# Loads of q and k on ScalarE's queue, and DMA work spread over the steps, in a threshold-attention and MLP kernel

## The chip, the cores and the metric

One core of one Trainium2 chip. The metric is the device time of one execution, in microseconds (us); the kernel before takes 534.13 us (median of 3 runs, 533.15 to 537.44). "Faster" or "slower" needs 2%.

## The reference, cut to what matters

```python
# q, k, v: (8 batches, 8 heads, 576 rows, 64), float32; tau = 0.02
scores = scale * q @ k^T
scores = where(scores >= max(scores) - tau, scores, -1e9)
attn   = softmax(scores);  x = attn @ v      # regrouped to 4608 x 512
out    = leaky_relu(x @ w_in) @ w_out        # 512 -> 2048 -> 512, slope 0.01
```

## The kernel before

The kernel runs 144 steps, 18 to a batch. A step forms scores of 128 query rows of a pair of heads (TensorE, L331), reduces them (VectorE, L391), thresholds and exponentiates them (GpSimd, ScalarE, VectorE); seven steps later the weights meet v. The MLP of earlier rows fills TensorE in between. q and k are loaded as float32 and split into two float16 halves by ScalarE and GpSimd.

Three things must be turned by 90 degrees by DMA transposes, all issued from the sync queue (SP in the profile): the halves of k (`kst<-ks`) and of q (`qst<-qs`), two of each a batch, and the attention weights (`wt<-w`), nine a batch and thirteen in the last. The same queue issues the loads of k and q and the stores of the result. GpSimd's queue has the loads of v, w_in and w_out. The lines that the change touches:

```python
LOADS = (-4, 3)
WOUT = 0

def load_half(src, store, nm, b, hb):
    m = store[b, hb] = sb.tile([128, 2, 576], FP32, tag=nm, bufs=2, name=nm)
    in_ = ...
    if nm == "km":
        nc.sync.dma_start(out=m, in_=...)                      # L100
    else:
        for f in range(2):
            nc.sync.dma_start(out=..., in_=in_[f])             # L103
...
def turn(nm, b, hb):
    nc.sync.dma_start(out=turned(...), in_=split_tile(...), transpose=True)   # L176
...
for b in range(1, B):
    s0 = 18 * (b - 1)
    for hb in range(2):
        t0 = s0 + (PREP1 if b < 2 else PREP)[hb]               # PREP = (3, 9)
        at(s0 + LOADS[hb], lambda ...: load_half(k, kms, "km", b, hb))
        at(s0 + LOADS[hb] + 1, lambda ...: load_half(q, qms, "qm", b, hb))
        ...
        at(t0 + 4, lambda ...: turn("k", b, hb))
        at(t0 + 7, lambda ...: turn("q", b, hb))
    for i in range(4):
        at(18 * b + i, lambda ...: load_v(b, i))               # GpSimd's queue
for g in range(8):
    at(WOUT + g // 2, lambda g=g: load_w_out(g))               # GpSimd's queue
...
    nc.sync.dma_start(out=uwt[now]..., in_=W_..., transpose=True)   # wt<-w, L540
```

`at(s, f)` runs f at the end of step s.

## Time and profile before

| | before |
|---|---|
| time, median | 534.13 us |
| span of the profiled run, granted clock | 529.1 us, 0.948 |
| TensorE's waits for DMA transposes | 13.7 us (wt) + 9.1 us (turns of q) |
| wt transposes, issue: median / mean / longest | 3.66 / 3.79 / 10.63 us |
| what the sync queue spends on issuing | 433.7 us: 381.4 on 104 transposes, 52.2 on loads and stores |

An issue is the time for which a queue is held by one DMA; landing is counted from its start to its completion. Two more views of before are needed later. First the DMA issues of the page (number, KB each, median us from issue to landing):

```profile
km<-in_k_dram SPq DMA_DIRECT2D x16, 576.0 KB, 4.7
qm<-in_q_dram SPq DMA_DIRECT2D x32, 288.0 KB, 4.7
...
wt<-w SPq DMA_TRANSPOSE x76, 6.6
```

Then the DMA queues of the page (packets, MB, time of their packets as a share of 16 engines' span). One queue, q1, carries all transposes, loads of k and q, and stores; q0 is GpSimd's:

```profile
q1 hardware_dynamic: 266304, 92.03, 90.4%
q0 software_dynamic: 13056, 8.92, 13.2%
```

### The profile page before, as it was taken

To read this page: it belongs to the slowest core of one execution; us is meant where nothing else is said; L and a number is where in the kernel's file an instruction comes from. 1 tells how busy PE (TensorE), PEld (TensorE's weight loads), DVE (VectorE), ACT (ScalarE), POOL (GpSimd) and SP (SyncE) were. 2 spreads that over 40 slices of the span, in tenths; PEclk is the share of its full clock that TensorE was granted. 3 is DMA by queue.
4 is the path that set the end of the run, shared out by engine and by line. 5 is a ranking of instruction groups with operands and counts; after the bars stand their busy time and mean duration, and the time that the engine had idled before them with its cause. 6 is when DMAs were issued, how large, how long until landed. Compare 5 with 4: busy or idle time off the path is not lost.

```text
span 529.1 us, 13454 instructions
## 1 busy us (share of the span) xinstructions
PE 475.8 (90%) x4912; PEld 294.5 (56%) x4912; DVE 464.1 (88%) x1213; ACT 424.6 (80%) x924; POOL 278.6 (53%) x476
## 2 busy tenths in 40 slices
PE   4666887999899997999999988999699999999996
PEld 3323454655565664656565655666455666656673
DVE  4985897999999997999999997999779999999542
ACT  6786888988999887898989897898859888878341
POOL 5575845675577645674567545764546644222000
PEclk9655798999999998999999999999989999999999
DMA  8999999999999999999999999999999999766301
GB/s 248 217 198 241 208 205 206 223 201 207 208 238 206 185 211 202 219 224 226 205 218 198 187 228 216 245 197 212 171 254 181 169 187 180 152 116 135 91 21 59
DMA packets 279425, 101.79 MB, mean 192 GB/s; under 512 B 254272, under 2 KB 266560, under 8 KB 279360
## 3 DMA queue, kind: packets, MB, share of 16 engines
q1 hardware_dynamic: 266304, 92.03, 90.4%
q0 software_dynamic: 13056, 8.92, 13.2%
q8 instruction: 38, 0.62, 0.5%
q14 instruction: 27, 0.22, 0.2%
HBM read 36.70 MB, written 9.44 MB: 87 GB/s over the span
## 4 chain that ended last, share of the span: by engine, by line
DVE 51%; DMA 15%; PE 14%; issue 12%; POOL 5%; ACT 2%; SPq 0%; POOLq 0%; DVEq 0%; ACTq 0%
DVE sf L391 20%; DMA wt<-w 10%; DVE gT L216 9%; DVE P L546 8%; DVE w L536 5%; PE op L236 5%; DMA qst<-qs 4%; PE hp L236 4%; PE sc L331 3%; DVE osb L272 3%; DVE xT L372 3%; POOL P L517 2%; PE pv L362 2%; POOL bb L515 1%; DVE rc L534 1%
## 5 line engine op out<-in xcount | busy, mean ns | idle before, releaser
L391 DVE TENSOR_SCALAR_CACHE_REDUCE sf<-sc 128x576 f32<-128x576 f32 x288 | 205.1, 747 | 15.6 <-PE sc L331 14.2
L551 ACT ACTIVATE w<-P 128x576 f16<-128x576 f16 x288 | 193.8, 674 | 8.6 <-DVE P L546 3.9
L331 PE MATMUL sc<-kst,qst 64*128 64x320 f16 (+1 forms) x1536 | 137.8, 300 | 26.1 <-DVE sf L391 16.2
L516 ACT ACTIVATE P<-sf,bb 128x576 f16<-128x576 f32 x144 | 111.3, 773 | 60.4 <-POOL bb L515 56.2
L236 PE MATMUL hp<-xT,win 128*128 128x256 f16 (+1 forms) x1344 | 152.3, 260 | 0.0
L236 PE MATMUL op<-wout,gT 128*128 128x512 f16 x576 | 150.8, 386 | 1.6 <-DVE osb L272 1.6
L236 PEld LDWEIGHTS <-win 128*128 128x128 f16 x1344 | 118.0, 99 | 44.0 <-issue 3.5
L331 PEld LDWEIGHTS <-qst 64*128 64x128 f16 x1536 | 75.9, 98 | 77.8 <-issue 48.2
L517 POOL TENSOR_SCALAR P<-sf,bb 128x576 f16<-128x576 f32 x139 | 105.9, 762 | 14.3 <-POOL bb L515 0.4
L216 DVE SCALAR_TENSOR_TENSOR gT<-hp,gT 128x512 f16<-128x512 f32 x144 | 98.2, 682 | 14.0 <-ACT gT L250 14.0
L250 ACT ACTIVATE gT<-hp 128x512 f16<-128x512 f32 x144 | 83.6, 581 | 20.5 <-PE hp L236 20.4
L515 POOL TENSOR_SCALAR bb<-mx 128x2 f32<-128x2 f32 x139 | 27.4, 197 | 120.9 <-DVE sf L391 107.7
L546 DVE TENSOR_SCALAR P<-P 128x1152 int16<-128x1152 int16 x144 | 82.0, 570 | 0.0
L236 PEld LDWEIGHTS <-gT 128*128 128x128 f16 x576 | 46.2, 98 | 64.3 <-issue 29.1
L362 PE MATMUL pv<-wt,v 128*64 128x256 f16 (+2 forms) x1000 | 56.8, 253 | 13.9 <-DMA wt<-w 13.7
L362 PEld LDWEIGHTS <-v 128*64 128x64 f16 x1000 | 38.2, 112 | 30.5 <-issue 26.3
L551 ACT ACTIVATION_READ_ACCUMULATOR w<-P 128x1 f32 x288 | 53.9, 187 | 0.0
L164 POOL TENSOR_TENSOR ks<-km,ks 128x320 f16<-128x320 f32 (+1 forms) x56 | 39.9, 733 | 10.8 <-DVE P L546 10.1
L372 DVE TENSOR_TENSOR xT<-pv,wt 128x128 f16<-128x128 f32 x128 | 31.7, 291 | 13.6 <-PE pv L362 13.5
L164 POOL TENSOR_TENSOR qs<-qm,qs 128x576 f16<-128x576 f32 x28 | 35.9, 1282 | 13.6 <-DVE P L546 13.6
L536 DVE TENSOR_SCALAR w<-rc 128x256 f16<-128x256 f32 (+1 forms) x76 | 39.6, 521 | 2.6
L126 POOL DMA_DIRECT2D v<-in_v_dram x32 | 20.6, 644 | 22.9 <-PE sc L331 10.1
(35 smaller groups left out, 211.8 us busy)
## 6 DMA issues: line engine op xcount, KB each, us to landing
km<-in_k_dram SPq DMA_DIRECT2D x16, 576.0 KB, 4.7
qm<-in_q_dram SPq DMA_DIRECT2D x32, 288.0 KB, 4.7
out_dram<-osb SPq DMA_DIRECT2D x36, 256.0 KB, 3.5
v<-in_v_dram POOLq DMA_DIRECT2D x16, 160.0 KB, 6.1
v<-in_v_dram POOLq DMA_DIRECT2D x16, 128.0 KB, 6.3
win<-in_moe_w_in_dram POOLq DMA_DIRECT2D x8, 256.0 KB, 10.1
wout<-in_moe_w_out_dram POOLq DMA_DIRECT2D x8, 256.0 KB, 11.0
wt<-w SPq DMA_TRANSPOSE x76, 6.6
```

Of the source, the lines that this page charges most:

```text
L164: return nc.gpsimd.tensor_tensor(out=dst[:, h], in0=src[:, h], in1=h_[:, h], op=AX.subtract)
L216: nc.vector.scalar_tensor_tensor(out=G.g[u], in0=hp, scalar=0.01, in1=G.g[u], op0=AX.mult, op1=AX.add)
L236: nc.tensor.matmul(out=out_, lhsT=lhsT, rhs=rhs, start=start, stop=stop, skip_group_check=True)
L250: nc.scalar.activation(out=G.g[u], in_=hp, func=AF.Relu, bias=0.0, scale=0.99)
L331: nc.tensor.matmul(out=sc[h][:, cols], lhsT=qt[r, qi, ds(2 * c, 2)].rearrange("d t a b -> d (t a b)")[:, g::2], rhs=rhs, start=(i == 0), s ...
L362: nc.tensor.matmul(out=o_[ds(64 * h, 64)], lhsT=vt[:, pp, h, j, :], rhs=w_[:, :, 4 * h + j, :], start=(j == 0), stop=(j == 4), skip_group_ ...
L391: nc.vector.tensor_scalar(out=sf, in0=sc[h][:, ds(SC0, 576)], scalar1=C, scalar2=None, op0=AX.mult, op1=AX.max, accum_out=mx[:, h : h + 1])
L516: nc.scalar.activation(out=P_[:, 1, :], in_=sB, func=AF.Identity, bias=bb[:, 1:2], scale=1.0)
L517: (nc.vector if s < SPOOL else nc.gpsimd).tensor_scalar(out=P_[:, 0, :], in0=sa, scalar1=1.0, scalar2=bb[:, 0:1], op0=AX.mult, op1=AX.add)
L536: nc.vector.tensor_scalar(out=W_[:, :, 1152:1280].rearrange("p i (h r) -> p i h r", h=2), in0=rc[:, 0:nw, :].unsqueeze(3).to_broadcast([12 ...
L546: anchor[0] = nc.vector.tensor_scalar(out=pi, in0=pi, scalar1=NEG, scalar2=None, op0=AX.max)
L551: nc.scalar.activation(out=uW[ui][:, i, ds(576 * h, 576)], in_=P_[:, h, :], func=AF.Exp, bias=exp_bias, scale=1.0, accum_out=usm[ui][:, i, ...
```

## The change

Its intent: take the loads of q and k off the crowded sync queue, and place loads, turns and the loads of w_out so that few DMAs fall on one step. The diff, cut to its core:

```diff
-    WOUT = 0
-    LOADS = (-4, 3)
+    LOADS = ((-6, 0), (2, 4))
+    TURNS = ((8, 10), (14, 16))
+    VS = (-6, 0, 2, 4)
+    WOUTS = (0, 2, 4, 6, 8, 10, 12, 14)
...
-            nc.sync.dma_start(out=m, ...)
+            nc.scalar.dma_start(out=m, ...)
...
-                nc.sync.dma_start(out=m.rearrange(...)[f], in_=in_[f])
+                nc.scalar.dma_start(out=m.rearrange(...)[f], in_=in_[f])
...
-            at(s0 + LOADS[hb], ... load_half(k, ...))
-            at(s0 + LOADS[hb] + 1, ... load_half(q, ...))
+            at(s0 + LOADS[hb][0], ... load_half(k, ...))
+            at(s0 + LOADS[hb][1], ... load_half(q, ...))
...
-            at(t0 + 4, ... turn("k", b, hb))
-            at(t0 + 7, ... turn("q", b, hb))
+            at(s0 + TURNS[hb][0], ... turn("k", b, hb))
+            at(s0 + TURNS[hb][1], ... turn("q", b, hb))
...
-            at(18 * b + i, ... load_v(b, i))
+            at(18 * b + VS[i], ... load_v(b, i))
...
-        at(WOUT + g // 2, ... load_w_out(g))
+        at(WOUTS[g], ... load_w_out(g))
```

More of the change, by code (lines that the diff above doesn't have):

```diff
@@ L99, in load_half @@
         if nm == "km":
-            nc.sync.dma_start(out=m, in_=in_.rearrange("f p h x -> (f p) h x"))
+            nc.scalar.dma_start(out=m, in_=in_.rearrange("f p h x -> (f p) h x"))
         else:
             for f in range(2):
-                nc.sync.dma_start(out=m.rearrange("(p f) h x -> f p h x", f=2)[f], in_=in_[f])
+                nc.scalar.dma_start(out=m.rearrange("(p f) h x -> f p h x", f=2)[f], in_=in_[f])
     anchor = [None]
@@ L458 @@
             t0 = s0 + (PREP1 if b < 2 else PREP)[hb]
-            at(s0 + LOADS[hb], lambda b=b, hb=hb: load_half(k, kms, "km", b, hb))
-            at(s0 + LOADS[hb] + 1, lambda b=b, hb=hb: load_half(q, qms, "qm", b, hb))
+            at(s0 + LOADS[hb][0], lambda b=b, hb=hb: load_half(k, kms, "km", b, hb))
+            at(s0 + LOADS[hb][1], lambda b=b, hb=hb: load_half(q, qms, "qm", b, hb))
             at(t0 - 1, lambda b=b, hb=hb: hi("k", b, hb))
@@ L471 @@
                             at(t0 + i, lambda nm=nm, h=h, b=b, hb=hb, part=part: after_anchor(lo(nm, b, hb, h, part)), ptick)
-            at(t0 + 4, lambda b=b, hb=hb: turn("k", b, hb))
-            at(t0 + 7, lambda b=b, hb=hb: turn("q", b, hb))
+            at(s0 + TURNS[hb][0], lambda b=b, hb=hb: turn("k", b, hb))
+            at(s0 + TURNS[hb][1], lambda b=b, hb=hb: turn("q", b, hb))
         for i in range(4):
-            at(18 * b + i, lambda b=b, i=i: load_v(b, i))
+            at(18 * b + VS[i], lambda b=b, i=i: load_v(b, i))
     for g in range(8):
-        at(WOUT + g // 2, lambda g=g: load_w_out(g))
+        at(WOUTS[g], lambda g=g: load_w_out(g))
     pv_at = {}
```

## The prediction

> **What bounds the kernel now.** I read the table of engines first, then the busy times in stretches, then the waits, then the sync queue in order of time.
>
> ```profile
> PE 475.8 (90%) x4912; PEld 294.5 (56%) x4912; DVE 464.1 (88%) x1213; ACT 424.6 (80%) x924; POOL 278.6 (53%) x476
> ```
>
> No engine is idle for long. I cut the steady part at the first score reduction (DVE, L391) of every sixth of the 144 steps. A batch is 18 steps, so three stretches are one batch; these are the batch from 187.3 us:
>
> ```profile
> 187.30:210.00 22.70, 19.76 (x174) 11.48 (x173) 18.97 (x51) 18.09 (x40) 10.23 (x19) 0.92 1.30 203
> 210.00:228.70 18.70, 18.70 (x208) 11.56 (x207) 18.31 (x50) 16.87 (x39) 13.74 (x22) 1.00 1.15 220
> 228.70:247.50 18.80, 18.65 (x199) 11.60 (x198) 18.70 (x52) 16.80 (x38) 11.62 (x19) 1.00 1.07 209
> ```
>
> Columns after the length: PE, PEld, DVE, ACT, POOL busy us, clock, DMA, GB/s. In the second and third stretch VectorE and TensorE are both full: a floor of 18.7 us for six steps. The first stretch is 4.0 us longer with no more VectorE work. Who held it:
>
> ```profile
> PE pv L362 <- DMA wt<-w: 13.7, 8, 4.5
> ...
> PEld L331 <- DMA qst<-qs: 10.6, 5, 3.2
> PE sc L331 <- DMA qst<-qs: 9.1, 4, 2.9
> ```
>
> (The list of waits: us in total, times, longest.) PE's waits for transposed tiles are 13.7 + 9.1 = 22.8 us in twelve places. The PEld line is mostly the same wait seen by the weight loads, and I don't add it. The place in the stretch above:
>
> ```profile
> 201.13 1.62 PE L331 MATMUL sc<-kst,qst 64*128 64x320 f16 x12 [2.94 <-DMA qst<-qs]
> ```
>
> ```profile
> 202.79 0.76 DVE L391 TENSOR_SCALAR_CACHE_REDUCE sf<-sc 128x576 f32<-128x576 f32 x1 [2.93 <-PE sc L331]
> ```
>
> PE stood for 2.94 us for the turned q, and VectorE behind it for 2.93. The chain of waits says the same ("190.78 10.31 DMA qst<-qs"). Why was q late? The sync queue before it:
>
> ```profile
> 179.94 2.71 SPq L176 DMA_TRANSPOSE kst<-ks  x1
> 182.71 0.58 SPq L100 DMA_DIRECT2D km<-in_k_dram  x1
> 183.39 0.58 SPq L273 DMA_DIRECT2D out_dram<-osb  x1
> 184.14 5.15 SPq L540 DMA_TRANSPOSE wt<-w  x1
> 189.34 1.34 SPq L103 DMA_DIRECT2D qm<-in_q_dram  x2
> 190.78 4.78 SPq L176 DMA_TRANSPOSE qst<-qs  x1
> 195.73 5.28 SPq L540 DMA_TRANSPOSE wt<-w  x1
> 201.10 0.60 SPq L273 DMA_DIRECT2D out_dram<-osb  x1
> 201.87 7.76 SPq L540 DMA_TRANSPOSE wt<-w  x2
> 209.69 0.58 SPq L100 DMA_DIRECT2D km<-in_k_dram  x1
> ```
>
> Each entry starts within 0.2 us of the end of the one before: the queue never waits for data, it is behind. The turn of q at 190.78 us was placed in step 16 of its batch and is issued in step 1 of the next, three steps late; it lands 0.04 us before PE's wait ends. So the steady state has two floors of nearly equal height: VectorE with TensorE at 3 x 18.7 = 56.1 us a batch, and the issue time of the sync queue. From medians that is 9 x 3.66 (wt) + 2 x 2.79 (kst) + 2 x 3.46 (qst) + 2 x 0.58 + 4 x 0.64 (loads) + 4.5 x 0.59 (stores) = 51.8 us, and about 21 gaps of 0.13 us make 54.6; in the batch above, with its slow transposes, I sum 57.6 us of issuing. When contention lifts it over 56, the queue falls behind and PE pays.
>
> **What the Trainium skill says.** "DMA: Bandwidth & Descriptors", section "Issuing engines are not separate DMA queues": DMAs of all engines run on the same 16 DMA engines, so another issuer saves only issue time. Issue time is what is short here (the rows above), so that is the right currency; bandwidth is not gained. "Perfetto Trace Analysis", section "DMA Instruction — HWDGE (DVE, Sync)": the descriptor generator is shared and locked for exclusive use, and the recorded time includes the wait for the lock. This trace has one hardware issuer alone and can't show it; it is my main risk. "ScalarE: Activation LUTs", section "What ACT_TABLE_LOAD costs": about 1283 ns; the trace agrees, 1.28 us at 0.80 us. "Advanced Engine Details and Errata", section "Sequencer Loop": engine instructions are queued, so a sequencer can be ahead of its engine. The trace agrees: ScalarE's sequencer passed the semaphore for a split (L154) at 139.59 us; that split started at 140.93, 1.34 us later.
>
> **The change part by part.**
>
> 1. Loads leave the sync queue. Per batch 2 x 0.58 + 4 x 0.64 = 3.7 us and six gaps (0.4): the 54.6 become 50.5, and the bad 57.6 some 53.5. Both are under 56.1, so the backlog drains and the transposes go out near their steps. The bytes stay, so contention stays.
>
> 2. Turns. k moves from steps 7 and 13 to 8 and 14; q stays at 10 and 16 (in the first batch prepared so, the first k turn stays at 8 and the first q turn moves from 11 to 10). The attention weights' transposes fall on odd steps, so all turns now lie between them. The queue stood behind no unready turn in the steady part, so this alone is worth little: 0 to 2 us overall.
>
> 3. Loads of w_out go from two a step in steps 0 to 3 to one every second step to step 14. The first wt was issued at 25.43 us, landed 16.57 us later beside them, and PE waited 4.51 us for it at 42.14. w_out pieces land about 1.5 us apart (29.41, 30.96, 32.68); four of the six that landed from 32.68 to 41.14 fall away from this window: about 6 us earlier, more than the 4.5 us wait. But k and q of the next batch now go out early and take some of that. I count 4 us.
>
> 4. The steady gain. Of the 22.8 us, 4.5 is the first wt (part 3) and 1.25 + 0.76 lie at 466 and 490 us, where nothing is loaded any more. 16.3 us remain, in six batches. I count 13, since v loads and both k and q still share the first six steps with the turn of q.
>
> 5. ScalarE pays. It gets the 3.7 us a batch. Its order is exp, exp, split, load; at the end of a step the sequencer is 1.3 us ahead, as much as a pair of q loads (1.28). So most is hidden if an issue still takes 0.6 us. But in the first six steps ScalarE is busy 17.83 of 19.00 us in an undisturbed batch (130.4 us), and 1.28 + 0.58 + 1.28 = 3.1 us fall just there. If half is exposed, 1.6 us meets 1.2 us of idle time and the 1.34 us by which ScalarE's relu usually precedes its reader on VectorE: nearly nothing comes through. I count 0.4 us a batch, 3 us.
>
> 6. The start. ScalarE's queue has the table load first:
>
> ```profile
> 0.80 1.28 ACT L70 ACT_TABLE_LOAD   x1 [0.80 <-PEq L593]
> 2.10 0.20 ACT L70 ACTIVATE warm<-warm 128x1 f32<-128x1 f32 x1
> 4.79 1.26 ACT L154 ACTIVATE ks<-km 128x640 f16<-128x640 f32 x2 [2.50 <-DMA km<-in_k_dram]
> ```
>
> The first load went out from the sync queue at 0.81 us; behind the table load it goes out at about 2.1 us. Everything at the start hangs on it: +1.3 us.
>
> Sum: 534.1 - 4 - 13 - 1 (turns) + 3 + 1.3 = 520.4 us, -2.6%.
>
> **Rivals.**
>
> A. The lock. If ScalarE's issue waits until the sync queue's transpose has generated its descriptors (3 to 5 us, and the sync queue issues nearly always), a load waits some 2 us on average, the second of a q pair again. Per batch in the first six steps 2 x 5 + 2.6 = 12.6 us instead of 3.1, less 3 x 1.3 hidden and 2.5 slack: 6 us of stall a batch, some 36 in six. Then 520 - 3 + 36 = about 553; milder, 530 to 545. For it: the skill's wording. Against it: the DMA page names the saving of issue time as the one use of a second issuer, and loads on the sync queue took 0.58 us right behind a transpose whose bytes were still in flight. I give a clearly lengthened issue one chance in four.
>
> B. The transposes are slowed by bandwidth, not by their queue. They take 3.1 us at best and 5.2 beside loads. If loads from a separate queue slow them as much or more, the queue drains less and the turn of q stays late: half of the 13 us is lost, about 527. For it: the DMA share over 1 in all steady stretches. Against it: the same stretches move 200 to 235 GB/s, while the first loads land 288 KB in 0.73 to 0.84 us, about 350 to 400 GB/s. One in four.
>
> C. Another engine is the bound anyway. VectorE's idle time from 12.6 to 483.7 us sums to 32.6 us, but only the 22.8 us of DMA waits are the change's to win: 534.1 - 22.8 = 511 us is the limit. ScalarE at 51.8 us a batch plus 3.7 makes 55.5, just under the floor of 56.1, so a third engine then stands level with the other two.
>
> **Range and chances.** Without A and B 514 to 522; with B 523 to 530; with A 530 to 555. The middle lands at 521, the range of 8 in 10 is 512 to 545. Faster by over 2% means under 523.4: half. Slower means over 544.8, only full A: 0.16. Within: 0.34.
>
> **What would show it.** Part 1: gaps of over 1 us in the sync queue, and turns of q issued in step 16 or 17. Parts 3 and 4: PE's waits for qst and wt under 6 us together, and stretches of six steps of 19 us. Part 5: ScalarE's load issues at 0.6 us; if their median is over 2 us, A holds and I am wrong on the sign. Part 6: the first split of k at about 6.1 us in place of 4.79. If the wt transposes' median issue rises over 4 us, B holds.

## The result, and the profile after

The changed kernel takes 565.0 us (median of 4 runs, 561.48 to 570.24), beside 535.79 us for the kernel before. The ratio is 1.052 (95% interval 1.043 to 1.061): slower. Ratios here are the mean time of one kernel's fast runs over that of the other's in the same rounds, so not quite the ratios of the medians quoted. The profiled run of the changed kernel was its slowest, 570.24 us (span 568.4); its three fast runs have spans of 559.6 to 563.4 us. (One core runs here; "slow" means a run over 1.5% above the fastest of the same kernel.) Where a size matters I also use an experiment that isolates the queue (act_only). A second series of the changed kernel:

**after_again** (the same kernel once more).

> The changed kernel once more, unchanged, for a profile in the fast state: 561 to 566 us by the earlier fast runs, with the same shape: wt transposes issuing in over 10 us in the first six steps of a batch, load issues on ScalarE of 0.4 to 0.7 us.

Measured: 564.2 us (554.56 to 577.41), ratio 1.041 (1.031 to 1.050). The loss repeats. Two of its four runs were slow, and its profile again fell in one of them:

```profile
PE pv L364 <- DMA wt<-w: 48.4, 15, 11.9
...
PE sc L333 <- DMA qst<-qs: 8.1, 1, 8.1
```

Now the trace. Line numbers in the changed kernel are two higher. Its waits (us in total, times, longest):

```profile
PE pv L364 <- DMA wt<-w: 52.7, 16, 12.5
...
PE sc L333 <- DMA qst<-qs: 1.9, 1, 1.9
```

The waits for the turned q, 9.1 us before, have all but gone in this run (after_again has one of 8.1 us). The waits for the attention weights' transposes went from 13.7 to 52.7 us. Together 22.8 became 54.6 us, 31.8 more; the span is 39.3 us longer. (TensorE was also busy for 484.2 us in place of 475.8, at a granted clock of 0.927 in place of 0.948.)

The same cut as the prediction's, by every sixth step (length, then busy us of PE, PEld, DVE, ACT, POOL, clock, DMA share, GB/s), in the batch that lost most:

```profile
147.40:168.80 21.40, 18.33 (x167) 11.14 (x166) 18.69 (x50) 17.90 (x39) 9.59 (x18) 0.92 1.23 155
168.80:202.70 33.90, 21.18 (x206) 12.60 (x205) 19.50 (x50) 17.49 (x40) 13.63 (x22) 0.80 1.11 154
202.70:221.40 18.70, 18.70 (x231) 12.44 (x230) 18.60 (x50) 16.05 (x37) 12.58 (x20) 1.00 1.12 209
```

The last stretch is at the floor of 18.7 us. The middle one is 15 us above it, with hardly more work on VectorE; the time of the DMA packets fills the 16 engines (share 1.11) and yet they move 154 GB/s, where the stretches of before that the prediction shows moved 203 to 220. What was issued there, each in order of time: the sync queue, then ScalarE's, then TensorE's wait.

```profile
149.93 3.91 SPq L542 DMA_TRANSPOSE wt<-w  x1
153.93 0.60 SPq L275 DMA_DIRECT2D out_dram<-osb  x1
154.69 31.65 SPq L542 DMA_TRANSPOSE wt<-w  x3
```

```profile
150.40 0.63 ACTq L105 DMA_DIRECT2D qm<-in_q_dram  x1
151.07 0.87 ACTq L105 DMA_DIRECT2D qm<-in_q_dram  x1
156.57 0.38 ACTq L102 DMA_DIRECT2D km<-in_k_dram  x1
163.46 0.64 ACTq L105 DMA_DIRECT2D qm<-in_q_dram  x1
165.99 0.61 ACTq L105 DMA_DIRECT2D qm<-in_q_dram  x1
```

```profile
182.80 1.28 PE L364 MATMUL pv<-wt,v 128*64 128x64 f16 x40 [12.51 <-DMA wt<-w]
```

The row of three spans 31.65 us: the first transpose was issuing for 15.51 us and the second for 12.14, where the median is 3.7. The third went out when all these loads had landed, and took 3.18. In each case the weights to be turned had been ready before the issue began, so this is not a wait for data. k was issued while both pieces of the q before it were in flight (they landed at 160.84 and 163.26 us), and the next q while k was (178.62 us); three v loads came from GpSimd meanwhile. TensorE stood 12.51 us for a transposed tile. The landing times of that window tell how slow everything was:

```profile
qm<-in_q_dram ACTq DMA_DIRECT2D x4, 288.0 KB, 14.4
km<-in_k_dram ACTq DMA_DIRECT2D x1, 576.0 KB, 22.0
...
wt<-w SPq DMA_TRANSPOSE x4, 13.9
```

Over the whole run the loads land later, the wt transposes at the median do not (6.7 beside 6.6 us); it is the tail that grew (longest issue 15.5, longest landing 28.1 us):

```profile
km<-in_k_dram ACTq DMA_DIRECT2D x16, 576.0 KB, 6.7
qm<-in_q_dram ACTq DMA_DIRECT2D x32, 288.0 KB, 8.4
...
wt<-w SPq DMA_TRANSPOSE x76, 6.7
```

And the queues of the page:

```profile
q1 hardware_dynamic: 257344, 73.15, 80.9%
q0 software_dynamic: 13056, 8.92, 12.3%
q10 hardware_dynamic: 8960, 18.88, 12.2%
```

The loads of k and q (8960 packets, 18.88 MB) have moved to a queue of their own, q10. q1 and q10 together are the very packets and bytes of before, but their time went from 90.4% of 529.1 = 478 us to 93.1% of 568.4 = 529 us. (Shares over 1, as in the stretches above, show that a packet's time includes time in which it stands still.)

So my first theory, **M**: loads on a second hardware queue run among the packets of the transposes, both slow down, and the transposes hold up the sync queue for longer than the removed loads had. Rivals: **S**, the new schedule does it (steps of loads, turns, w_out); **V**, the v loads that now share steps with the k and q loads do it; **E**, ScalarE or other engines, busy beside the transfers, do it.

### The profile page after: what moved, and what is told of

Its sections match the earlier page's. It is cut to its first block, busy times and chain, and to the rows that moved or that the text cites. A ratio compares the mean times of both kernels' runs of the same rounds, so it can differ in the third digit from the quotient of the medians.

```text
span 568.4 us, 13448 instructions
## 1 busy us (share of the span) xinstructions
PE 484.2 (85%) x4912; PEld 299.0 (53%) x4912; DVE 465.1 (82%) x1213; ACT 423.1 (74%) x924; POOL 279.0 (49%) x476
## 3 DMA queue, kind: packets, MB, share of 16 engines
q10 hardware_dynamic: 8960, 18.88, 12.2%
## 4 chain that ended last, share of the span: by engine, by line
DVE 39%; DMA 25%; PE 14%; issue 11%; POOL 6%; ACT 2%; ACTq 0%; POOLq 0%; DVEq 0%
DMA wt<-w 24%; DVE sf L393 15%; DVE gT L218 8%; DVE P L548 7%; PE op L238 5%; DVE w L538 3%; PE hp L238 3%; PE sc L333 3%; POOL P L519 3%; DVE osb L274 2%; PE pv L364 2%; DVE xT L374 2%; ACT w L553 1%; POOL bb L517 1%; POOL ks L166 1%
## 5 line engine op out<-in xcount | busy, mean ns | idle before, releaser
L393 DVE TENSOR_SCALAR_CACHE_REDUCE sf<-sc 128x576 f32<-128x576 f32 x288 | 205.2, 748 | 21.3 <-PE sc L333 18.6
L333 PE MATMUL sc<-kst,qst 64*128 64x320 f16 (+1 forms) x1536 | 139.7, 306 | 17.6 <-DVE sf L393 15.2
L519 POOL TENSOR_SCALAR P<-sf,bb 128x576 f16<-128x576 f32 x139 | 107.2, 771 | 14.2 <-POOL bb L517 0.2
L333 PEld LDWEIGHTS <-qst 64*128 64x128 f16 x1536 | 75.4, 100 | 70.3 <-issue 47.6
L517 POOL TENSOR_SCALAR bb<-mx 128x2 f32<-128x2 f32 x139 | 27.1, 195 | 166.2 <-DVE sf L393 156.8
L364 PE MATMUL pv<-wt,v 128*64 128x256 f16 (+2 forms) x1000 | 59.2, 261 | 54.2 <-DMA wt<-w 52.7
L548 DVE TENSOR_SCALAR P<-P 128x1152 int16<-128x1152 int16 x144 | 84.2, 585 | 0.2 <-POOL P L519 0.2
L364 PEld LDWEIGHTS <-v 128*64 128x64 f16 x1000 | 41.3, 118 | 70.1 <-issue 65.7
L374 DVE TENSOR_TENSOR xT<-pv,wt 128x128 f16<-128x128 f32 x128 | 31.8, 292 | 28.3 <-PE pv L364 28.2
L166 POOL TENSOR_TENSOR ks<-km,ks 128x320 f16<-128x320 f32 (+1 forms) x56 | 39.8, 729 | 10.3 <-DVE P L548 9.6
L538 DVE TENSOR_SCALAR w<-rc 128x256 f16<-128x256 f32 (+1 forms) x76 | 37.1, 488 | 2.6
```

The source lines that it names most:

```text
L166: return nc.gpsimd.tensor_tensor(out=dst[:, h], in0=src[:, h], in1=h_[:, h], op=AX.subtract)
L333: nc.tensor.matmul(out=sc[h][:, cols], lhsT=qt[r, qi, ds(2 * c, 2)].rearrange("d t a b -> d (t a b)")[:, g::2], rhs=rhs, start=(i == 0), s ...
L364: nc.tensor.matmul(out=o_[ds(64 * h, 64)], lhsT=vt[:, pp, h, j, :], rhs=w_[:, :, 4 * h + j, :], start=(j == 0), stop=(j == 4), skip_group_ ...
L393: nc.vector.tensor_scalar(out=sf, in0=sc[h][:, ds(SC0, 576)], scalar1=C, scalar2=None, op0=AX.mult, op1=AX.max, accum_out=mx[:, h : h + 1])
L519: (nc.vector if s < SPOOL else nc.gpsimd).tensor_scalar(out=P_[:, 0, :], in0=sa, scalar1=1.0, scalar2=bb[:, 0:1], op0=AX.mult, op1=AX.add)
L538: nc.vector.tensor_scalar(out=W_[:, :, 1152:1280].rearrange("p i (h r) -> p i h r", h=2), in0=rc[:, 0:nw, :].unsqueeze(3).to_broadcast([12 ...
```

## The experiments

Seventeen kernels ran beside the kernel before. Medians of before moved between 532.24 and 537.08 us (a single run beside mix_phase took 528.05), so I read ratios.

**1. even_sync: the change with its queue undone.**

```diff
-            nc.scalar.dma_start(out=m, ...)      # both load sites
+            nc.sync.dma_start(out=m, ...)
```

> The changed kernel with one part undone: the q and k loads are issued from the sync queue again, the new steps stay. Theory M (mixing: packets of loads from a second queue between the packets of a transpose slow both down): the collapse goes, the time is 534 us or less, I guess 525, and the first transpose of weights in a batch issues in under 6 us. Rival S (the new steps are the harm, three loads and three v loads in steps 0 to 4): stays near 560 us. Rival I (issue on ScalarE costs): also falls, but then PE's waits for transposes would not have been the loss.

Measured: 533.47 us, ratio 0.999 (0.993 to 1.006). The schedule alone costs nothing and gains nothing in all. (In the profiled runs its first batch is 5.0 us longer than before's, 63.8 us, and the next six together 6.9 us shorter, 349.7 us.) Its waits:

```profile
PE pv L364 <- DMA wt<-w: 27.3, 20, 4.2
```

TensorE no longer stands for the turns of q (only 0.7 us of weight loads do), though the second one still goes out in step 0 or 1 of the next batch in all seven. The waits for wt doubled against before's 13.7 us, in many small places. So 4.5 us more of waiting in total came with no longer time: waits are a guide to a loss, not its exact size.

**2. act_only: before, with nothing changed but the queue of the q and k loads.**

```diff
-            nc.sync.dma_start(out=m, ...)        # both load sites
+            nc.scalar.dma_start(out=m, ...)
```

> The kernel before with the queue alone changed: q and k loads from ScalarE's queue, all steps as before. Theory M: slower than before by as much as the whole change or nearly, 550 to 570 us, with wt transposes of over 8 us to issue where a load is in flight. Rival S: within 1% of before, 530 to 538.

Measured: 553.11 us (549.35 to 557.2), ratio 1.034 (1.025 to 1.043):

```profile
PE pv L362 <- DMA wt<-w: 45.9, 16, 9.1
...
PE sc L331 <- DMA qst<-qs: 1.7, 2, 1.5
```

The queue alone brings the loss, on the old schedule too. Waits for wt plus turns are 47.6 us, 24.8 more than before, and its span (555.2 us) is 26.1 us longer: about as much. S as sole cause falls. What the sync queue spent, summed over its issues in each trace:

| us | all issues | 104 transposes | loads and stores |
|---|---|---|---|
| before | 433.7 | 381.4 | 52.2 |
| even_sync | 437.9 | 386.7 | 51.3 |
| act_only | 447.6 | 426.5 | 21.2 |
| after | 459.0 | 437.5 | 21.6 |

The change took 30.6 us of issuing off the queue, and the transposes that stayed there took 56.1 us more (45.1 more in the fast run of act_only). The queue that was to be relieved is held for longer.

**3. wout_only: before, with the loads of w_out spread as in the change.**

```diff
-        at(WOUT + g // 2, ... load_w_out(g))
+        at(WOUTS[g], ... load_w_out(g))          # (0, 2, 4, 6, 8, 10, 12, 14)
```

> The kernel before with the w_out loads alone spread to one every second step. My prediction's part 3 said 4 us off: 530 us, with PE's first wait for wt (4.51 us at 42 us) gone. Under theory M too, since those loads come from a second queue (GpSimd) and mix with the first transpose: the 10.6 us of its issue fall to 4 to 7.

Measured: 535.97 us, ratio 1.004 (0.997 to 1.010). The first wt transpose behaves as predicted, 10.63 us of issue before and now

```profile
25.67 5.80 SPq L540 DMA_TRANSPOSE wt<-w  x1
```

and the first batch shrinks from 58.8 to 53.4 us. But the second batch grows from 58.9 to 65.6 us, and the gain is given back at once. All w_out loads still go out and land in the first batch, so they are not what slows the second; why it grew was not isolated.

**4. mix_bench: loads and transposes of the kernel's shapes by themselves** (zeros go out; profile only).

```diff
+ 4 x wt<-w | loads alone | in turn on one queue | loads from ScalarE's queue, then transposes | v ...
```

> No attention at all (zeros go out, wrong on purpose): six phases with a barrier between, each twice: A four weight transposes (640 KB) alone, B four k loads (576 KB) alone, C both in turn on the sync queue, D the same with the loads from ScalarE's queue, E eight loads from two queues, F transposes beside four v loads of GpSimd's queue. Theory M: A about 14 us, B about 7, C about A + B = 21, D clearly more than C, 30 us or more, E about twice B, F more than A by over the v loads' own time. Rival: two queues only share, then D is C or less, and the harm in the kernel is one of order and not of mixing.

Measured, first issue to last landing in two passes: four transposes 14.5 and 14.3 us, four loads 8.4 and 8.8, in turn on one queue 22.5 and 22.9, loads from ScalarE's queue and transposes 21.3 and 21.4. No loss, but the loads were all started before the transposes and hardly met them, and the v part did not run as meant. Inconclusive.

**5 and 6. before_no_v and after_no_v: no v loads from the third batch on** (wrong result).

```diff
-            at(18 * b + VS[i], ... load_v(b, i))
+            at(18 * b + VS[i], ... load_v(b, i) if b < 2 else vts.__setitem__(b, vbufs[b % 2]))
```

> The kernel before without the v loads of batches 2 to 7 (stale v, wrong result on purpose). Theory M: these loads are what delays the turn of q at the start of a batch in the kernel before, so PE's waits for transposes fall from 22.8 us to under 9, the time to 518 to 522. Rival (the sync queue's own length delays it): within 1% of before.

> The changed kernel without the v loads of batches 2 to 7 (stale v, wrong result on purpose). Theory M with two queues enough for the collapse: still slower than the kernel before without them, 530 to 550 us. Rival (it takes three queues at once): falls to the level of the kernel before without v, some 515 us.

Measured: before without v 518.53 us, ratio 0.971 (0.965 to 0.977), with 11.8 us of waits for turned tiles where under 9 were expected; the change without v 543.35 us, ratio 1.009 (0.998 to 1.020). Waits for wt, before_no_v and then after_no_v:

```profile
PE pv L362 <- DMA wt<-w: 7.0, 2, 5.9
```

```profile
PE pv L364 <- DMA wt<-w: 28.4, 6, 13.3
```

Without v the old kernel runs at its floor from the third batch on (56.3 to 56.6 us), so v is worth 15 us there. The change stays 1.009 / 0.971 = 1.039 times as long as its counterpart, but this ratio does not clear v. In the profile of after_no_v, of a slow run, the batches take 73.7, 63.6, 60.8, 61.4 and then 56.3 to 56.6 us, and the first two still have v and w_out loads. In the five batches from the third on, the change is 9.3 us longer than its counterpart without v (two waits for wt, of 3.6 and 3.9 us), and 21.8 us with v. So v is not needed for a loss, but more than half of the later loss comes only with it.

**7. v_sync: v as float32 on the sync queue, cast by GpSimd.**

```diff
-            at(18 * b + i, ... load_v(b, i))                    # GpSimd's queue, cast in the DMA
+            at(18 * b + (-8, -7, 1, 1)[i], ... load_vf(b, i))   # sync queue, float32
+            at(18 * b + (-2, -1, 5, 5)[i], ... cast_v(b, i))    # GpSimd
```

> A right version meant to be better: the kernel before with v of batches 1 to 7 loaded as float32 from the sync queue and cast on GpSimd (two casts of 1024 and two of 256 columns), so that no second queue mixes with the transposes after the start. Theory M: gains most of what leaving v out gains, 520 to 526 us. Rival (sync queue's length): slower than before, over 536 us, since 2.4 us of issuing a batch come on.

Measured: 543.92 us, ratio 1.021 (1.012 to 1.029). Longer by 2.1%: with four more loads the sync queue issues 57 to 61 us a batch from the second on, over the floor of 56.1, which makes it the likely bound. M's forecast of 520 to 526 us failed, but the length of the queue is enough to explain that. So it decides nothing on M, and suggests that the queue's length matters, as the prediction had it.

**8. mix_stream: a stream of eight transposes, loads started by the landing of one of them** (zeros out; profile only).

> No attention (zeros go out, wrong on purpose). The earlier bench let the loads start before the transposes, so it hardly mixed them; here eight weight transposes stream from the sync queue and loads start in their midst: phase 1 none, 2 a q pair, k and a q pair in the same queue, 3 the same three from ScalarE's queue as transposes land, 4 four v loads from GpSimd's queue, 5 is 2 with 4, 6 is 3 with 4; each twice. Theory M: phase 1 about 27 us, 2 about 36, 3 at least 40 and more than 2, 4 over 33, 6 the longest, over 50. Rival (sharing without loss): 3 no longer than 2, 4 about 31, 6 about 38.

Measured, us from the first transpose to the landing of the last (a v load landed up to 1.3 us later), in two passes: transposes alone 27.3 / 27.5; q, k, q in the same queue 33.3 / 33.5; from ScalarE's queue 31.8 / 31.7; v from GpSimd 32.1 / 32.2; same queue and v 40.1 / 37.5; ScalarE's and v 36.8 / 36.4. M in its simple form, any mixing costs, falls: single loads beside transposes lose nothing.

**9. even_v_early: the even schedule on the sync queue, v loads moved to steps -11, -9, -7, -5.**

```diff
-    VS = (-6, 0, 2, 4)
+    VS = (-11, -9, -7, -5)
```

> New steps with q and k on the sync queue, and the v loads moved to steps 7, 9, 11 and 13 of the batch before, where fewest other loads go. If it matters what v meets: 522 to 529 us, PE's waits for wt from 27 us to under 15. If v costs the same wherever it meets transposes (they always run): 530 to 536, same as before.

Measured: 544.22 us, ratio 1.014 (1.007 to 1.021), outside both forecasts; waits for wt 37.6 us in 25 places. With v away from the steps of q and k it is longer than the same schedule before (0.999), not shorter. So spreading is not good in itself.

**10 to 12. stores_act, stores_pool, even_stores_pool: only the stores leave the sync queue.**

```diff
-            return lambda: nc.sync.dma_start(out=G.rows[i], in_=osb)
+            return lambda: nc.scalar.dma_start(out=G.rows[i], in_=osb)   # stores_act
+            return lambda: nc.gpsimd.dma_start(out=G.rows[i], in_=osb)   # stores_pool, even_stores_pool
```

> The kernel before with the stores of the result from ScalarE's queue. They take 3 us of the sync queue's issue a batch. If mixing harms with stores as with loads: slower, 540 us or more. If only loads from HBM harm: 520 to 527, as the sync queue gets its slack.

> The same with the stores from GpSimd's queue. Same two outcomes: 540 us or more if mixing harms with stores, 520 to 527 if not; the difference to the run before tells whether the kind of second queue matters.

> A right version meant to be best: new steps, q and k on the sync queue, stores from GpSimd's queue. The stores alone gave 1.3% on the old steps. If the sync queue's length bounds the new steps too: 522 to 529 us. If v's mixing bounds them: 530 to 536.

Measured: stores_act 538.78 us, ratio 1.004 (0.998 to 1.010), between its two forecasts; stores_pool 529.94 us, ratio 0.987 (0.980 to 0.995); on the even schedule 532.66 us, 0.998 (0.991 to 1.005). So use of ScalarE's queue is not harmful as such: stores there cost nothing. On the old schedule stores from GpSimd gain 1.3%, the fastest correct version that I ran, ahead of both kernels, but under the 2% that counts as faster. Its waits for wt are 9.2 us; those for turns of q stay at 9.0:

```profile
PE pv L362 <- DMA wt<-w: 9.2, 7, 5.0
```

**13. mix_busy: the stream again, with stores and with busy engines** (zeros out; profile only).

> The stream bench again (zeros go out, wrong on purpose), each phase with eight transposes and the q, k, q loads: from the same queue, from ScalarE's queue, and from ScalarE's queue with four v loads; without and with three stores between the transposes; and all that once with idle engines and once with VectorE, ScalarE, GpSimd and TensorE busy on tiles of their own; at the end ScalarE's queue with stores and one engine busy at a time. If the engines' own traffic is what turns sharing into collapse: with idle engines 31 to 37 us a phase as before, with busy ones the ScalarE-queue phases 45 us or more and the same-queue phase under 40. If the stores do it: the collapse shows with idle engines in the phases with stores. If neither: all phases stay within 15% of the earlier bench and the order of issue in the kernel is what is left.

Measured (sync queue / ScalarE's queue / ScalarE's and v): idle engines 34.7 / 33.7 / 38.5 us, with stores 36.4 / 34.2 / 39.1, all engines busy 34.8 / 31.8 / 36.6, both 36.7 / 34.0 / 39.8. Neither busy engines nor stores make the second queue lose: E falls as far as a bench can tell.

At this point two benches contradicted the kernels. Reading the four traces with loads on ScalarE's queue again, I saw an order: a load of q or k that started with no other load (q, k, v) in flight, over 2.4 us into a transpose's issue, landed in 3.6 to 6.0 us (15 loads); one started earlier in 4.2 to 11.8 (27 loads, median 5.9); and one that met other loads in 4.2 to 22.0 (118 loads, median 8.7). The benches' start signal had let every load go singly and at about 2 us into an issue. Hence theory **P**: it is loads piled up on the second queue that crawl with the transposes.

**14. mix_phase: the moment and the piling varied apart** (zeros out; profile only).

```diff
+ for n in (1, 800, 1600, 2300):   # singly, later and later after a landing
+     phase(ScalarE, n, pile=False)
+ phase(sync, pile=True)           # q, k, q at once behind one transpose
+ phase(ScalarE, 1, pile=True); phase(ScalarE, 1600, pile=True)
+ ... and the three piles again with the v loads
```

> A bench, zeros go out on purpose. Eight transposes stream on the sync queue; q, k and q loads of the kernel's own shapes come beside them. What is read is the time of a phase from the first transpose to the last landing. Phases: transposes alone (27.4 us expected from the bench before); loads in the same queue (33.4); loads from ScalarE's queue, each started by the landing of a transpose, at once or some 0.8, 1.6 or 2.4 us later, so that they meet the next transposes at another moment; all three loads at once behind one transpose, from the sync queue and from ScalarE's, at once and 1.6 us later; and the last three with the four v loads as well. Theory P (the moment or the piling up decides: loads that start when a transpose has just begun, or that meet other loads in flight, crawl and hold the transposes): at least one of the ScalarE phases is over 5 us longer than the sync queue's phase of the same loads, and loads in it land after 8 us or more. Theory Q (neither moment nor piling up matters in itself, the loss needs something else of the kernel): all ScalarE phases lie within 3 us of their sync counterpart, loads land in under 8 us.

Measured, both passes:

| us | phase | q and k landing, slowest |
|---|---|---|
| transposes alone | 27.1 / 27.3 | |
| singly, sync queue | 33.6 / 33.4 | 4.4 / 4.8 |
| singly, ScalarE's, four moments | 31.0 to 32.9 | 5.7 to 7.7 |
| pile, sync queue | 33.3 / 33.3 | 5.9 / 6.3 |
| pile, ScalarE's, at once | 37.9 / 36.5 | 14.6 / 12.6 |
| pile, ScalarE's, a write of 1600 elements later | 31.0 / 31.1 | 7.0 / 7.3 |
| pile with v, sync queue | 37.9 / 35.9 | 8.7 / 6.5 |
| pile with v, ScalarE's, at once / later | 38.0, 37.3 / 35.4, 34.6 | 9.5, 9.2 / 9.4, 9.1 |

The collapse is there in one row, in both passes: a pile on ScalarE's queue, 4.6 and 3.2 us over the same pile on the sync queue. The transposes in it, the sync queue's pile first (three transposes, the loads, and the one transpose behind them):

```profile
224.94 9.44 SPq L59 DMA_TRANSPOSE wt<-w  x3
234.41 1.26 SPq L68 DMA_DIRECT2D qm<-in_q_dram  x2
235.72 0.60 SPq L63 DMA_DIRECT2D km<-in_k_dram  x1
236.77 1.28 SPq L68 DMA_DIRECT2D qm<-in_q_dram  x2
238.10 5.26 SPq L59 DMA_TRANSPOSE wt<-w  x1
```

and ScalarE's, its loads and the two transposes that met them:

```profile
268.97 1.47 ACTq L68 DMA_DIRECT2D qm<-in_q_dram  x2
270.56 0.55 ACTq L63 DMA_DIRECT2D km<-in_k_dram  x1
271.20 2.62 ACTq L68 DMA_DIRECT2D qm<-in_q_dram  x2
```

```profile
270.02 16.96 SPq L59 DMA_TRANSPOSE wt<-w  x2
```

Two transposes take 16.96 us for some 6.3, and k, issued 0.5 us into one, lands after 14.4 us. In the same queue one transpose is held to 5.26 us and the rest run free. The two phases by queue, the sync queue's first:

```profile
q1 hardware_dynamic: 21584, 7.01, 101.7%
```

```profile
q1 hardware_dynamic: 20736, 5.24, 91.1%
q10 hardware_dynamic: 848, 1.77, 19.9%
```

The same 21584 packets take 101.7% of 33.3 = 33.9 us in one queue, and 111% of 37.9 = 42.1 us in two; in the later pile (87.7 + 15.6)% of 31.0 = 32.0 us. It is a minority of packets that crawls: from 270 to 287 us the median packet of a transpose (256 bytes) took 18 ns and that of a load (2304 bytes) 93 ns, just as in the sync queue's pile, but the slowest 5% took over 193 and 696 ns, where they took over 18 and 149. So two queues do not slow down by being two. They do when several loads meet transposes at one moment, and not at another. The excess is under the 5 us that I had asked of P, over the 3 us that I had left Q. And where v, on a third queue, joins the pile, the sync queue's pile is as slow (37.9 / 35.9 us) as ScalarE's: the trouble is not ScalarE's alone.

**15 and 16. after_apart and sync_apart: the piles taken out of the kernel.** Each load of k, half of q and part of v gets a step of its own, with q and k on ScalarE's queue as in the change, or on the sync queue as a control.

```diff
-    LOADS = ((-6, 0), (2, 4))
-    VS = (-6, 0, 2, 4)
+    LOADS = ((-7, (-4, -2)), (1, (3, 5)))     # k, (first half of q, second half)
+    VS = (-5, -1, 2, 4)
```

> The changed kernel with its ten loads of a batch each in a step of its own: k, each half of q and the four v loads no longer share a step; ScalarE's queue stays. The bench has shown that three loads at once from ScalarE's queue behind a transpose crawl for 12 to 15 us and hold transposes for 15 us, where single ones don't. Theory P (piling up makes the loss): the waits for wt fall under 25 us (52.7 in the changed kernel), no wt issue over 9 us, k and q land in a median of under 5.5 us; 530 to 543 us, ratio to before under 1.02. Theory R (the second queue costs it however the loads are spread): 550 us or more, waits for wt over 40 us.

> The control: the same spread with q and k loads on the sync queue. Under both theories it stays near the even schedule on the sync queue, 530 to 538 us, ratio 0.99 to 1.01. If it moves by more, the spread itself does something, and what the other run shows has to be read against this one.

Measured: after_apart 548.57 us (543.28 to 550.85), ratio 1.024 (1.015 to 1.033); sync_apart 544.86 us, ratio 1.023 (1.013 to 1.033). The waits of after_apart, then of sync_apart:

```profile
PE pv L366 <- DMA wt<-w: 34.9, 11, 7.5
```

```profile
PE pv L366 <- DMA wt<-w: 30.9, 15, 6.1
```

| loads of q and k | on the sync queue | on ScalarE's queue | two queues over one |
|---|---|---|---|
| schedule of before | 1.000 | 1.034 | 3.4% |
| the change's schedule | 0.999 | 1.052 and 1.041 | 5.3% and 4.2% |
| each load in its own step | 1.023 | 1.024 | 0.1% |

Ratios to before, each with a 95% interval of about 0.01 either way, so that the last column is good to some 1.3%. In the last row the mean of all fast runs gives 547.8 to 543.2 us, 0.9%. So with the loads spread, what the second queue costs is inside the noise, and clearly less than on the other two schedules. TensorE's waits for turned weights and q in the profiled runs tell where (the first batch ends at the first score reduction of the second):

| us | first batch | after it |
|---|---|---|
| before, act_only | 4.5, 9.1 | 18.3, 38.6 |
| even_sync, after | 10.1, 15.1 | 17.1, 39.6 |
| sync_apart, after_apart | 12.6, 20.7 | 22.0, 19.8 |

After the first batch the second queue adds 20.3 and 22.5 us of waits on the two piled schedules and none (-2.2) on the spread one. There, too, fewer loads started with two or more others in flight: 6 of 33 in after_apart, 18 of 35 in the change. In the first batch, where GpSimd loads w_in and w_out as well, the second queue still adds 8.1 us with the loads of q and k spread. after_apart also took v out of their steps, so it shows what piles of q, k and v together do, not q and k alone.

The control was needed: the spread itself costs 2%, so after_apart missed all numbers of P (34.9 us of waits for under 25, a longest wt issue of 10.92 us for under 9, landings of 5.6 us for k and 6.5 for q at the median for under 5.5, 548.57 us for 543 at most), and without sync_apart I would have put that on the queue. Theory R (550 us or more, waits over 40 us) was missed, too. In the accounts of the sync queue, transposes take 419.1 us in after_apart and 397.9 in sync_apart: 21 us more, and 30 us of loads fewer. There the trade comes out about even. With the change's piles it is 437.5 to 386.7, 51 us more for the same 30.

**What stays open.** First, what inside the DMA engines makes a pile crawl at one moment and not at another. The Trainium skill, "DMA: Bandwidth & Descriptors", section "Queues, rings and completion order", says that sync and ScalarE queues each own a row of rings on the same 16 engines, and that an engine takes rows in turn, a whole packet at a time. The two rows are in the traces (q1 and q10), and a load behind a transpose in one ring against one that shares the engines with it would fit; but no run here shows the taking of turns, nor why a minority of packets stands still. Second, the crawl in the kernel is longer than the bench's (28.1 us of landing beside 16.9). Third, why the spread of sync_apart costs 2% by itself (in its profile 6.2 of 9.0 us lie in the first batch, 65.0 us in place of 58.8). I did not isolate these.

## Why the prediction was wrong

By its steps:

- **Part 1, the sync queue is relieved: wrong in size and sign.** The loads left as counted (30.6 us over the run; 3.7 a batch), but the transposes on the queue took 56.1 us more. The step that failed reads "The bytes stay, so contention stays". Bytes and packets did stay; their time did not (478 to 529 us), and with nothing but the queue of the loads changed (act_only) the transposes took 45.1 us more. The queue's issuing in the five steady batches from 147.4 us on was 55.5 to 67.1 us, not 50.5 to 53.5. The sum had a slip of its own: 54.6 includes the gaps between issues and 57.6 does not. With some 2.7 us of gaps the bad batch stands at 60.2 us, its whole length, and less 4.1 it comes to 56.1, the floor itself and not under it.
- **Its test, "gaps of over 1 us in the sync queue, and turns of q issued in step 16 or 17": met in part.** The second turn of q goes out in step 17 in four of seven batches (one of seven before), and in step 0 or 1 of the next batch in the other three. The waits for turns fell from 9.1 to 1.9 us (8.1 in after_again); in even_sync they all but vanish with the old queue, so the schedule gives this, too. Gaps of over 1 us in the sync queue, none in before from 25 to 394 us, came in four places between 110 and 210 us and then not until 439 us. TensorE's waits were to be under 6 us together and were 54.6.
- **Part 2, turns: worth little, not contradicted.** Even_sync, which has them among other moves, is at 0.999; nothing ran with the turns alone.
- **Part 3, w_out, -4 us: a local gain of 5.4 us and a net of zero.** In wout_only the first wait for wt went, but the second batch was 6.7 us longer, for a reason not isolated.
- **Part 4, -13 us of 16.3: the main failure.** The waits for wt and turns rose by 31.8 us (24.8 in the fast run of the queue alone). I took TensorE's DMA waits as an upper limit to a gain, and let them only fall, because I let the issue of a transpose keep its length when the loads left its queue. It did not: 3.79 us in the mean became 4.55 (4.27 in act_only).
- **Part 5, ScalarE pays 3 us: about right, as far as it can be seen.** Its load issues have medians of 0.38 us (k) and 0.63 us (q), less than the 0.58 and 0.64 us on the sync queue. Nothing points to a part of the loss from them.
- **Part 6, the start, +1.3 us: wrong, 0.** ScalarE's sequencer issued the first load while its engine loaded the table:

```profile
0.80 1.28 ACT L72 ACT_TABLE_LOAD   x1 [0.80 <-PEq L595]
0.97 0.44 ACTq L102 DMA_DIRECT2D km<-in_k_dram  x1
```

  The first split started at 4.78 us, as before (4.79). The prediction had itself noted, with a trace beside it, that a sequencer can be ahead of its engine, and did not apply it here.
- **Rival A, the lock: false.** 36 load issues began inside a transpose's issue, and took 0.63 us at the median and 1.43 at most. It was the one path by which the prediction allowed for a clear loss (0.16).
- **Rival B, "the transposes are slowed by bandwidth, not by their queue": the right direction, given one in four and a size of half of 13 us.** It was sized by bandwidth, and argued against by 350 to 400 GB/s for loads alone. The loss came in phases of 154 GB/s at a DMA share of 1.11, so free bandwidth was no argument. My test for it, a median wt issue over 4 us, missed it too: the median is 3.71 us, and the mean went from 3.79 to 4.55 us by its tail. For waits, the tail is what to ask for.
- **Rival C** did not come into play.

The shown part: the queue is the cause (even_sync and act_only, two schedules), the loss is in waits for wt, and spreading the loads takes it away after the first batch, within the noise (after_apart with its control). Argued only: whether it is the second queue as such or the moment at which it lets the loads start, which no kernel run held fixed; that q and k alone can make the pile there, as v was spread with them; whether the 2% that the spread itself costs hides a rest of the loss; and how the engines take packets of two queues.

## What to carry to other kernels

Moving loads off a queue that also issues DMA transposes can cost more than it saves: in the bench several loads at once from a second queue stretched two transposes from some 6 us to 17, at one moment and not at another. So count, on top of the issue time saved, what the remaining transposes may take longer, from the mean and tail of their issues and not the median; try first what is small and comes singly (the stores here, on GpSimd's queue, gave -1.3%, "unclear", on the old schedule and nothing on the new). And a schedule experiment needs its control on the old queue, since spreading alone moved the time by 2%.

## What the Trainium skill lacked or had wrong

- "DMA: Bandwidth & Descriptors", section "Issuing engines are not separate DMA queues", says that issuing from several engines only saves issue time. Here it also cost: with q and k loads on ScalarE's queue, the transposes on the sync queue took 437.5 us of issue in place of 386.7 on the same schedule, and the kernel 4 to 5% more time.
- The same page, section "Rules for kernel authors", says that a transpose next to ordinary DMAs needs nothing. That holds for correctness (after_again and act_only gave right results); for time, a pile of loads from a second queue made two transposes take 16.96 us, where the same pile in their own queue held one to 5.26 us.
- "Perfetto Trace Analysis", section "DMA Instruction — HWDGE (DVE, Sync)", lets one expect that a second issuer waits for the lock while descriptors are generated. The 36 load issues of ScalarE that began inside a transpose's issue, of 3 to 15 us each, took 0.63 us at the median and 1.43 at most; a lock for the length of a transpose was not seen.
- That a DMA issue can overtake the activation table load on ScalarE's queue is said by no page that I read in so many words; the general rule that the prediction quotes, that a sequencer can be ahead of its engine, covers it. The issue went out at 0.97 us, within the load from 0.80 to 2.08 us.
